# Gated linear attention and an ELU feed-forward layer on one core: blocks of 384 tokens instead of 256 from the fourth block on

## The chip, the cores and the metric

The kernel runs on one core of a Trainium2 chip. The metric is the device time of one execution in microseconds (us). The kernel before took 470.91 us, the median of three runs (469.48 to 471.95).

## The reference

Four sequences of 768 tokens pass through a linear attention of 8 heads of 48 with a gate for each step, and the 3072 resulting rows of 384 numbers through a feed-forward layer of width 2048. All arrays are float32.

```python
for t in range(S):                                   # S = 768, for every sequence b and head h
    state = alpha[:, :, t, :, None] * state + k_t (outer) v_t      # 48 x 48
    y[:, :, t] = q_t @ state
x = y.transpose(0, 2, 1, 3).reshape(3072, 384)
h = x @ w_in                                         # 384 x 2048
g = where(h > 0, h, exp(min(h, 0)) - 1)
out = g @ w_out                                      # 2048 x 384
```

## The kernel before, in words

**Tiling.** The attention works in 24 windows of 128 tokens (6 to a sequence), the feed-forward layer in 12 blocks of 256 tokens, two windows each. Every float32 product of the layer is made of three products in fp32r: each operand is split in an upper part and a rest, and rest times rest is left out.

**Steps.** The program is written as tokens, one small function each, called with a window or with a block `b` and a step `j`. A token issues its instructions on the engines' queues, and each queue runs in the order of the tokens. For a window: `L`, `LV` load it, `SC` scans the gates (VectorE), `LN`, `EX`, `PC` are ScalarE's, `KA`, `KB`, `KC`, `SQ` scale k and q (GpSimd and VectorE), `T` transposes k on VectorE in four parts of four instructions (line 296), `S` makes the scores (line 335) and `U` the products of k and v (line 380) on TensorE, both into two banks called q, `MK` masks the scores (line 363), `UA`, `UB`, `UC` bring the state forward (lines 417, 446), `Y` makes the rows of y (line 464; `YL`, `Y3` and `XP` help in the first four windows), and `XH`, `XL`, `XD` write them, split, into the block's tile `xt`.

For a block, the 2048 features are cut in 8 steps `j` of 256. `A(b, j)` (line 656) makes h for 256 features and 256 tokens: 2 groups of 128 features, 9 matmuls each of 256 columns (3 parts of the 384 inputs, 3 products each), both groups in one bank. `RA`, `RB` (lines 673, 678, ScalarE) make exp(min(h, 0)), `RC` (line 684, VectorE) the activation g, `GH` (line 690, ScalarE) its upper part, `GL` (line 704; VectorE, for the pairs in the table `GQS` GpSimd) the rest. `O(b, j)` (line 718) multiplies by w_out: for each of 2 groups of 128 tokens 6 matmuls of 384 columns, summed over all `j` in one bank per group, so two banks of the eight. `Z` (lines 727, 730) copies the two banks out, through tiles `ot` of which there are two, and stores them; the last block's stores go out on ScalarE's queue, the others on SyncE's.

**Order.** The string `START` writes out the tokens of blocks 0 to 3 with their windows and the arrival of the weights (`F` loads a piece, `KW`, `DA`, `DB`, `WH`, `WL` unpack and split it). After it `steady()` repeats the string `STEADY` once per block. The string `BANKS` gives the PSUM bank of every tile in turn, and a tile waits until the one before it in its bank is done with.

```python
def steady(g0=4):
    for g in range(g0, g0 + 10):
        for x in STEADY.split():
```

Of the kernel before, what the change touches and what calls it, by code (L numbers as in the profile page):

```python
# [24 lines left out]
NBLK = B * S // BLK  # L25
# [14 lines left out]
WLV, KAV, KBV, SQV = (0, 1, 2, 3, 4, 7, 8, 9, 13, 14, 15), (0, 1, 2, 6), (0, 1, 2, 3, 4, 10), (0, 1, 3, 6, 10)  # L40
# [3 lines left out]
GQS = ((0, 1), (0, 4), (0, 5), (0, 6), (0, 7), (1, 1), (1, 5), (1, 7), (2, 1), (2, 3), (2, 4), (2, 5), (2, 7), (3, 0), (3, 2), (3, 3), (3, 4))  # L44
# [9 lines left out]
DB.2 WH.4 A.0.0 RA.0.0 ZV.6 TP.3 DA.1 WL.4 KN.3 F.7 DA.3 WH.6 PC.2 XP.2 LV.3 RB.0.0 UC.2 S.3 MK.3 U.3 L.4 KW.3 A.0.2  # L54
WL.6 UA.3 F.10 YL.3 F.9 Y3.3 RC.0.0 GH.0.0 RA.0.2 XL.2 RB.0.2 DB.1 RA.0.1 SC.4 DB.3 F.8 Y.3 XH.3 RB.0.1 XL.3 RC.0.1
LV.6 F.12 A.0.3 WH.1 SQ.4 WH.5 WL.5 DA.4 GH.0.1 KW.4 F.14 A.1.0 UB.3 GL.0.1 GL.0.0 LV.5 RC.0.2 GH.0.2 RA.1.0 WL.1 WH.3
A.1.1 LN.4 EX.4 RB.1.0 GL.0.2 L.5 PC.3 A.1.3 UC.3 RA.1.1 WL.3 DB.4 RA.1.3 SC.5 RC.1.0 WH.8 WL.8 RB.1.1 A.1.2 RA.1.2
RB.1.2 SQ.5 RC.1.1 O.0.0 O.0.1 O.0.2 RC.1.2 KA.4 A.1.4 KB.4 F.11 RB.1.3 RC.1.3 GH.1.1 GH.1.0 GL.1.0 GL.1.1 O.1.0 WH.7
DA.5 WL.7 RA.0.3 RB.0.3 RC.0.3 WH.10 LN.5 O.1.1 GH.1.2 GL.1.2 O.1.2 EX.5 KC.4 GH.0.3 GL.0.3 O.0.3 DA.6 RA.1.4 GH.1.3
RB.1.4 GL.1.3 LC.1 WL.10 LV.7 A.0.5 KA.5 KB.5 KW.5 DB.5 KW.6 RA.0.5 A.0.4 RB.0.5 DB.6 RC.1.4 WH.11 RA.0.4 RB.0.4 O.1.3  # L60
RC.0.4 GH.1.4 GH.0.4 RC.0.5 WH.9 KC.5 A.1.5 WL.11 RA.1.5 WH.12 S.4 GL.1.4 RB.1.5 PC.5 S.5 GL.0.4 TP.4 KN.4 WL.12 WL.9
RC.1.5 L.6 GH.1.5 O.0.4 MK.5 U.4 WH.14 TP.5 PC.4 L.7 GH.0.5 GL.0.5 MK.4 O.1.4 SC.6 KN.5 F.13 LN.6 EX.6 WL.14 A.1.7
# [12 lines left out]
TB.10 GL.3.3 GL.3.4 O.2.7 KC.11 TB.11 TA.11 LC.4 L.12 Z.2 PC.10 LV.11
# [20 lines left out]
def gla_elu_ffn(ctx: ExitStack, tc: tile.TileContext, qka, vv, vn, wgt, out):  # L96
# [84 lines left out]
    @tok  # L181
    def L(i):
        t = qtile(i)
        nc.sync.dma_start(out=t, in_=qka[i, :, 0:QW])
# [282 lines left out]

    def xs(i):
        blk, half = divmod(i, 2)
        if blk not in xt:  # L470
            xt[blk] = xpool.tile([128, 2, NC, 2, W], F32R, name="xt", tag="xt")
        return xt[blk][:, half]
# [180 lines left out]

    @tok
    def A(b, j):
        x = xt[b]
        h = bank("h").rearrange("p (f x) -> p f x", f=2)
        ff[b, j] = dict(h=h)
        for f in range(2):
            k = 0  # L660
            t = wgts[2 * j]
            for c in range(NC):
                ws = slice(f * DM + c * 128, f * DM + c * 128 + 128)
                for wi, xi in ((0, 0), (0, 1), (1, 0)):
                    nc.tensor.matmul(h[:, f, :], lhsT=t[:, wi, ws], rhs=x[:, :, c, xi].rearrange("p a x -> p x a"),  # L665
                                     start=(f == 0 and k == 0), stop=(k == 8), skip_group_check=True)
                    k += 1

    @tok
    def RA(b, j):  # L670
        d = ff[b, j]
        r = d["r"] = gpool.tile([128, 2, BLK], F32, name="r", tag="r", bufs=3)
        nc.scalar.activation(out=r, in_=d["h"], func=AF.Relu, scale=-1.0)  # L673
# [6 lines left out]
    @tok  # L680
    def RC(b, j):
        d = ff[b, j]
        d["g"] = d["r"] if (b, j) in GQS else d["h"]
        nc.vector.scalar_tensor_tensor(out=d["g"], in0=d["r"], scalar=-1.0, in1=d["h"], op0=ALU.add, op1=ALU.max)  # L684

    @tok
    def GH(b, j):
        d = ff[b, j]
        gh = d["gh"] = gpool.tile([128, 2, BLK], F32R, name="gh", tag="gh", bufs=3)
        nc.scalar.copy(out=gh, in_=d["g"])  # L690

    @tok
    def GP(b, j):
        rest(ff[b, j]["h"], ff[b, j]["gh"])

    @tok
    def GL(b, j):
        d = ff[b, j]
        gl = d["gl"] = gpool.tile([128, 2, BLK], F32R, name="gl", tag="gl", bufs=3)
        if (b, j) in GPE:  # L700
            nc.scalar.copy(out=gl, in_=d["h"])
        else:
            q = nc.gpsimd if (b, j) in GQS else nc.vector
            q.tensor_tensor(out=gl, in0=d["g"], in1=d["gh"].bitcast(F32), op=ALU.subtract)  # L704

    @tok
    def O(b, j):
        d = ff.pop((b, j))
        gh, gl = d["gh"], d["gl"]
        if j == 0:  # L710
            ops_[b] = [bank("o") for _ in range(2)]
        for m in range(2):
            o = ops_[b][m]
            ms = slice(m * 128, m * 128 + 128)
            for f in range(2):
                t = wgts[2 * j + 1]
                for k, (gt, wi) in enumerate(((gh, 0), (gh, 1), (gl, 0))):
                    nc.tensor.matmul(o[:, 0:DM], lhsT=gt[:, f, ms],  # L718
                                     rhs=t[:, wi, f * DM:f * DM + DM].rearrange("p (a x) -> p x a", a=2),
                                     start=(j == 0 and f == 0 and k == 0),  # L720
                                     stop=(j == NJ - 1 and f == 1 and k == 2))

    @tok
    def Z(b):
        for m in range(2):
# [4 lines left out]
            q.dma_start(out=out[b * BLK + m * 128:b * BLK + m * 128 + 128, :], in_=ot)  # L730
        del ops_[b], xt[b]
# [43 lines left out]
def steady(g0=4):  # L775


    p, steps, last = [], dict(A=29, RA=29, RB=29, RC=29, GH=29, GL=29, O=27), NBLK * NJ
    for g in range(g0, g0 + 10):
        for x in STEADY.split():  # L780
            x, k, *y = x.split(".")
            if x in steps:
                k = NJ * g + int(k)
                if steps[x] <= k < last:
                    p.append((x, *divmod(k, NJ)))
            elif x in ("CA", "CB", "LC"):
                k = 4 * g + int(k)
                if 4 + (x == "LC") <= k < 4 * NJ:
                    p.append((x, k))
            elif x == "Z":  # L790
                if g0 - 1 <= g + int(k) < NBLK:
                    p.append((x, g + int(k)))
            elif x in ("V", "VP"):
                if g == NBLK - 1:
                    p.append((x,))
            elif 2 * g + int(k) < NWIN:
                p.append((x, 2 * g + int(k), *map(int, y)))
    return p


def general(ctx, tc, ident, whi, wlo, flag, qka, vn, wgt, out):
# [4 lines left out]
    with tc.If(good < 1):  # L806
        with ExitStack() as st:
# [177 lines left out]
```

## Time and profile before

| | us |
|---|---|
| runs of the kernel before, median (lowest to highest) | 470.91 (469.48 to 471.95) |
| the profiled execution, its own time | 471.73 |
| its span, first to last instruction | 470.0 |
| TensorE busy in the span | 461.1 (98%) |
| VectorE busy | 369.2 (79%) |
| ScalarE busy | 314.6 (67%) |
| GpSimd busy | 133.9 (28%) |
| granted TensorE clock, mean | 0.998 of 2.4 GHz |

The span is what the profiler saw between the first and the last instruction; 1.7 us of the execution's time lie around it. Matmuls are pipelined, so the duration of one says little: what one costs is the distance from start to start in a row of them, which the chain of waits gives as the length of a piece divided by its count. The other engines' rows give the mean duration of an instruction.

### The profile page before, as it was taken

Reading aid. Unit: us, or ns where it says so; the run is one execution under the profiler, and the core shown is the slowest. Engines: PE = TensorE matmul, PEld = TensorE weight load, DVE = VectorE, ACT = ScalarE, POOL = GpSimd, SP = SyncE. Lnnn points to the kernel's source line nnn. Section 1 sums busy time; section 2 is a strip of 40 time slices with the busy share of each in tenths; the row PEclk is TensorE's granted clock in tenths of the full one; section 3 lists DMA queues with packets and bytes.
Section 4 is the critical chain, followed back from the end, with each engine's and each line's share of the span. In section 5 each row is a group of like instructions: output and inputs, shape, how many; then the busy total and the mean of one; then the engine's idle time right before and its main releaser. Section 6 shows DMA issues by size and latency. Waiting matters only on the chain.

```text
span 470.0 us, 13140 instructions
## 1 busy us (share of the span) xinstructions
PE 461.1 (98%) x5413; PEld 446.1 (95%) x5414; DVE 369.2 (79%) x763; ACT 314.6 (67%) x664; POOL 133.9 (28%) x114
## 2 busy tenths in 40 slices
PE   8999999999999999999999999999999999999994
PEld 3899999999999999999999999999999999999994
DVE  7899978797959889789889889789899897334430
ACT  4789988685746566866865875767775865663550
POOL 2116545265544414403502602602602500000000
PEclk9999999999999999999999999999999999999999
DMA  8999704414070175246227236326325222110001
GB/s 309 398 415 354 242 1 153 153 52 165 16 210 2 39 231 189 68 122 201 69 85 234 71 92 214 85 85 214 93 77 177 68 77 78 33 44 10 2 35 38
DMA packets 20482, 61.12 MB, mean 130 GB/s; under 512 B 2880, under 2 KB 7872, under 8 KB 20416
## 3 DMA queue, kind: packets, MB, share of 16 engines
q1 hardware_dynamic: 20128, 59.82, 38.4%
q8 instruction: 44, 0.72, 0.7%
q10 hardware_dynamic: 288, 0.39, 0.2%
q14 instruction: 22, 0.18, 0.1%
HBM read 53.52 MB, written 4.72 MB: 124 GB/s over the span
## 4 chain that ended last, share of the span: by engine, by line
PE 98%; DVE 0%; ACT 0%; issue 0%
PE h L665 42%; PE o L718 40%; PE y L464 4%; PE q L380 2%; PE q L335 2%; PE y L459 2%; PE wp L137 2%; PE sc L351 1%; PE tp L286 1%; PE y L504 1%; PE u L398 1%; PE yl L459 1%; PE u L424 0%; PE y L523 0%; PE xf L137 0%
## 5 line engine op out<-in xcount | busy, mean ns | idle before, releaser
L665 PE MATMUL h<-xt,w 128*128 128x256 f32 x1728 | 201.2, 276 | 0.0
L665 PEld LDWEIGHTS h<-xt,w 128*128 128x128 f32 x1728 | 197.6, 192 | 0.9
L718 PE MATMUL o<-w,gh 128*128 128x384 f32 x768 | 188.8, 328 | 0.0
L718 PEld LDWEIGHTS o<-w,gh 128*128 128x128 f32 x768 | 132.6, 189 | 0.8
L718 PE MATMUL o<-w,gl 128*128 128x384 f32 x384 | 125.3, 326 | 0.0
L673 ACT ACTIVATE r<-h 128x512 f32<-128x512 f32 x96 | 56.1, 596 | 55.2 <-PE h L665 52.9
L296 DVE STREAM_TRANSPOSE kn<-qka 32x128 f32<-32x128 f32 x256 | 77.5, 303 | 4.0
L684 DVE SCALAR_TENSOR_TENSOR h<-r,h 128x512 f32<-128x512 f32 x79 | 53.8, 692 | 26.6 <-ACT r L678 26.1
L718 PEld LDWEIGHTS o<-w,gl 128*128 128x128 f32 x384 | 72.6, 189 | 0.1
L704 DVE TENSOR_TENSOR gl<-h,gh 128x512 fp32r<-128x512 f32 x79 | 54.0, 689 | 18.6 <-ACT gh L690 15.8
L690 ACT CAST gh<-h 128x512 fp32r<-128x512 f32 x79 | 45.8, 579 | 32.1 <-DVE h L684 19.7
L235 POOL TENSOR_TENSOR qka<-qka,R 128x512 f32<-128x512 f32 x20 | 26.8, 1342 | 137.9 <-ACT R L227 101.8
L678 ACT ACTIVATE r<-r 128x512 f32<-128x512 f32 x96 | 60.4, 631 | 1.8
L265 POOL TENSOR_TENSOR st<-qka,P 64x512 f32<-64x512 f32 x32 | 40.7, 1271 | 27.0 <-DVE P L213 17.4
L363 DVE TENSOR_TENSOR st<-q,mask 64x256 f32<-64x256 f32 x72 | 30.3, 421 | 8.0 <-PE q L335 6.8
L213 DVE TENSOR_TENSOR_SCAN P<-qka,first 128x516 f32<-128x516 f32 x24 | 30.5, 1269 | 5.5 <-DMA qka<-in_qka_dram 5.1
L222 ACT ACTIVATE R<-P 128x512 f32<-128x512 f32 x24 | 15.1, 630 | 28.9 <-DVE P L213 28.9
L704 POOL TENSOR_TENSOR gl<-r,gh 128x512 fp32r<-128x512 f32 x17 | 24.4, 1438 | 25.8 <-ACT gh L690 18.6
L240 POOL TENSOR_TENSOR R<-P,R 128x512 f32<-128x512 f32 x18 | 23.3, 1296 | 10.9 <-DVE qka L235 9.6
L615 ACT ACTIVATE ck<-ck,lim 128x384 int32<-128x384 int8 x32 | 24.1, 755 | 2.2 <-DMA ck<-in_wgt_dram 2.2
L620 ACT ACTIVATE ck<-ck,lim 128x384 f32<-128x384 int32 x32 | 22.9, 715 | 0.8
L464 PEld LDWEIGHTS y<-st,vs 128*64 128x64 f32 x576 | 18.0, 138 | 2.5 <-issue 2.3
(95 smaller groups left out, 430.2 us busy)
## 6 DMA issues: line engine op xcount, KB each, us to landing
qka<-in_qka_dram SPq DMA_DIRECT2D x22, 770.0 KB, 6.1
ck<-in_wgt_dram SPq DMA_DIRECT2D x32, 384.0 KB, 3.6
raw<-in_wgt_dram SPq DMA_DIRECT2D x16, 767.6 KB, 9.8
vs<-in_vv_dram SPq DMA_DIRECT2D x36, 192.0 KB, 4.3
out_dram<-ot SPq DMA_DIRECT2D x22, 192.0 KB, 2.0
vs<-in_vv_dram SPq DMA_DIRECT2D x6, 384.0 KB, 7.0
xt<-y SPq DMA_DIRECT2D x40, 48.0 KB, 2.2
qka<-in_qka_dram SPq DMA_DIRECT2D x2, 512.0 KB, 5.0
```

Of the source, the lines that this page charges most:

```text
L213: nc.vector.tensor_tensor_scan(out=P.rearrange("p n w -> p (n w)"), data0=t[:, 2 * NP * W:], data1=first.rearrange("p n w -> p (n w)"), in ...
L265: eng(SQV, i).tensor_tensor(out=st[r, a], in0=d["q"][r], in1=pw(i)[r], op=ALU.mult)
L296: nc.vector.transpose(out=kn[32 * t:32 * t + 32, :, 32 * g:32 * g + 32], in_=d["kt"][32 * g:32 * g + 32, :, 32 * t:32 * t + 32])
L363: nc.vector.tensor_tensor(out=d["st"][r, a, :, c * C:(c + 1) * C], in0=d["s4"][a][o], in1=mask[o].unsqueeze(1).broadcast_to([64, NP, C]), ...
L464: nc.tensor.matmul(out[64 * a:64 * a + m], lhsT=lhs(i, c, a)[:, n * D:n * D + m], rhs=d["st"][:, a, n, c * C:(c + 1) * C], start=start, st ...
L665: nc.tensor.matmul(h[:, f, :], lhsT=t[:, wi, ws], rhs=x[:, :, c, xi].rearrange("p a x -> p x a"), start=(f == 0 and k == 0), stop=(k == 8) ...
L673: nc.scalar.activation(out=r, in_=d["h"], func=AF.Relu, scale=-1.0)
L678: nc.scalar.activation(out=d["r"], in_=d["r"], func=AF.Exp, scale=-1.0)
L684: nc.vector.scalar_tensor_tensor(out=d["g"], in0=d["r"], scalar=-1.0, in1=d["h"], op0=ALU.add, op1=ALU.max)
L690: nc.scalar.copy(out=gh, in_=d["g"])
L704: q.tensor_tensor(out=gl, in0=d["g"], in1=d["gh"].bitcast(F32), op=ALU.subtract)
L718: nc.tensor.matmul(o[:, 0:DM], lhsT=gt[:, f, ms], rhs=t[:, wi, f * DM:f * DM + DM].rearrange("p (a x) -> p x a", a=2), start=(j == 0 and f ...
```

## The change

From block 3 on a block has 384 tokens, three windows, so that there are 3 blocks of 256 and 6 of 384. In a wide block a step `j` is one group of 128 features: there are 16 steps, `A` makes one h of 128 x 384 with 9 matmuls of 384 columns, the elementwise tokens work on 128 x 384, and `O` has 3 groups of 128 tokens with 3 matmuls each, in three banks. The tables are rewritten: `STEADY` now holds one wide block, `START` holds blocks 0 to 2 and twelve steps of block 3, `BANKS` follows. In a wide block `GL` is GpSimd's for 5 of the 16 steps (`GQW`). Some of the early windows' `KA`, `KB`, `SQ` and some weights' `WL` change between VectorE and GpSimd. The tiles r, gh and gl, three of each before, share ten. `xt` is laid out in another order, so that a row that `XD` moves is cut in six pieces. The loads of the last four windows are issued in two parts. `Z` copies three banks, each as a token of its own. A fallback that does not run with these inputs (`general`) is rewritten for both widths.

```diff
+NARROW = 3
+WIDE = 384
+NBLK = NARROW + (B * S - NARROW * BLK) // WIDE
-WLV, KAV, KBV, SQV = (0, 1, 2, 3, 4, 7, 8, 9, 13, 14, 15), (0, 1, 2, 6), (0, 1, 2, 3, 4, 10), (0, 1, 3, 6, 10)
+WLV, KAV, KBV, SQV = (0, 2, 3, 4, 8, 10, 11, 12), (0, 1, 2, 4, 7, 8), (0, 1, 2, 3, 5, 9), (0, 1, 3, 5)
+GQW = (2, 5, 8, 11, 14)
...
-            xt[blk] = xpool.tile([128, 2, NC, 2, W], F32R, name="xt", tag="xt")
+            xt[b] = xpool.tile([128, NC, 2, WIDE], F32R, name="xt", tag="xt")
...
+    def parts(b, j):
+        return ((j // 2, j % 2),) if wide(b) else ((j, 0), (j, 1))
+    def gtile(b, dt, name):
+        return cut(b, gpool.tile([128, 512], dt, name=name, tag="g", bufs=10))
...
     def A(b, j):
-        for f in range(2):
+        for y, (p, f) in enumerate(parts(b, j)):
...
-                    nc.tensor.matmul(h[:, f, :], lhsT=t[:, wi, ws], rhs=x[:, :, c, xi].rearrange("p a x -> p x a"),
+                    nc.tensor.matmul(h[:, y, :], lhsT=t[:, wi, ws],
+                                     rhs=x[:, c, xi].rearrange("p (a x) -> p x a", a=2),
...
     def O(b, j):
-            ops_[b] = [bank("o") for _ in range(2)]
+            ops_[b] = [bank("o") for _ in range(2 + wide(b))]
...
-    def Z(b):
-        for m in range(2):
+    def Z(b, *ms):
+        for m in ms or range(2):
             ot = gpool.tile([128, DM], F32, name="ot", tag="ot")
             nc.scalar.copy(out=ot, in_=ops_[b][m][:, 0:DM])
```

**Where the instructions move.** TensorE, steady part, around the small products of the windows (q is written by `S`, line 335, and `U`, line 380; y by `Y`, line 464). Before, two windows' `Y` stand together, and elsewhere two windows' `U` and `S`:

```order
L718 MATMUL o<-w_695,gl 128x384
L464 MATMUL y<-st,vs_121 64x64 x16
L464 MATMUL y<-st,vs_120 64x64 x16
L665 MATMUL h<-xt,w_1070 128x256 x18
...
L380 MATMUL q<-vs_118,kn 48x48 x16
L335 MATMUL q<-st,qka_133 64x64 x16
L380 MATMUL q<-vs_119,kn 48x48 x16
L335 MATMUL q<-st,qka_134 64x64 x16
L718 MATMUL o<-w_1023,gh 128x384 x2
```

The same engine and part of the changed kernel, where `S` is line 349, `U` line 394, `Y` line 478, `A` line 701 and `O` line 747:

```order
L747 MATMUL o<-w_863,gl 128x384
L478 MATMUL y<-st,vs_120 64x64 x16
L349 MATMUL q<-st,qka_133 64x64 x16
L394 MATMUL q<-vs_121,kn 48x48 x16
L747 MATMUL o<-w_863,gh 128x384 x2
```

Each stop now serves one window's `Y` and another window's `S` and `U`, three stops to a wide block of three windows.

VectorE, steady part, the transposes `T` (kn, line 296) of two windows before the scores. Before:

```order
L704 TENSOR_TENSOR gl<-h,gh 128x512
L296 STREAM_TRANSPOSE kn<-qka_133 32x4x32 x4
L296 STREAM_TRANSPOSE kn<-qka_134 32x4x32 x4
L541 TENSOR_TENSOR y_4541<-y,y_4541 128x128
L545 TENSOR_TENSOR xt<-y,xt 128x3x128
```

The changed kernel, the transposes of the window whose `S` and `U` stand in the stop shown above (transposes line 310, `RC` line 721, `GL` line 734, `KC` line 259, `XL` line 568, `MK` line 377):

```order
L568 TENSOR_TENSOR xt<-y,xt 128x3x128
L259 SCALAR_TENSOR_TENSOR qka_133<-R,qka_133 128x512
L721 SCALAR_TENSOR_TENSOR h<-r,h 128x384
L310 STREAM_TRANSPOSE kn<-qka_133 32x4x32 x4
L734 TENSOR_TENSOR gl<-h,gh 128x384
L310 STREAM_TRANSPOSE kn<-qka_133 32x4x32 x4
L721 SCALAR_TENSOR_TENSOR h<-r,h 128x384
L734 TENSOR_TENSOR gl<-h,gh 128x384
L310 STREAM_TRANSPOSE kn<-qka_133 32x4x32 x4
L721 SCALAR_TENSOR_TENSOR r<-r,h 128x384
L734 TENSOR_TENSOR gl<-h,gh 128x384
L310 STREAM_TRANSPOSE kn<-qka_133 32x4x32 x4
```

The transposes now stand between the elementwise steps of the block, and the last four come right ahead of the stop that needs them.

ScalarE, the end of the program (copies and stores of the last block, with what each waits for; DMAHW is a DMA's semaphore). Before:

```order
L690 CAST gh<-h 128x512 [waits PE_49]
L727 COPY ot<-o 128x384 [waits DMAHW0_49,PE_49]
L730 DMA out_dram<-ot 128x384 [waits Activation_49]
L727 COPY ot<-o 128x384 [waits DMAHW1_49,PE_49]
L730 DMA out_dram<-ot 128x384 [waits Activation_49]
```

The changed kernel (copy line 757, store line 760):

```order
L757 COPY ot<-o 128x384 [waits DMAHW3_49,PE_49]
L760 DMA out_dram<-ot 128x384 [waits DMAHW5_49,Activation_49]
L757 COPY ot<-o 128x384 [waits DMAHW4_49]
L760 DMA out_dram<-ot 128x384 [waits DMAHW6_49,Activation_49]
L757 COPY ot<-o 128x384 [waits DMAHW5_49,PE_49]
L760 DMA out_dram<-ot 128x384 [waits Activation_49]
```

There is a third copy and store, and the third copy takes the `ot` tile of the first.

## Rows read from the trace of the kernel before

**Rows 1.** The page, busy time of each engine.

```profile
PE 461.1 (98%) x5413; PEld 446.1 (95%) x5414; DVE 369.2 (79%) x763; ACT 314.6 (67%) x664; POOL 133.9 (28%) x114
```

**Rows 2.** Waits of TensorE, the one past its start: waiter, releaser, us in total, times, longest.

```profile
PE y L504 <- ACT y L492: 0.4, 1, 0.4
```

**Rows 3.** Chain that ended last: start us, length us, what, matmuls.

```profile
57.84 2.28 PE o L718 x14
...
262.23 7.80 PE o L718 x48
270.03 2.02 PE y L464 x64
272.05 6.22 PE h L665 x54
...
280.22 0.51 PE q L380 x32
...
447.89 6.03 PE h L665 x54
...
463.68 0.03 issue
```

**Rows 4.** Timeline of TensorE at the start of a stop: start us, length us.

```profile
269.71 0.33 PE L718 MATMUL o<-w,gl 128*128 128x384 f32 x1
269.96 0.28 PE L464 MATMUL y<-st,vs 128*64 128x64 f32 x2
```

**Rows 5.** Groups by form: busy us, mean ns of one, idle before.

```profile
L678 ACT ACTIVATE r<-r 128x512 f32<-128x512 f32 x96 | 60.4, 631 | 1.8
L690 ACT CAST gh<-h 128x512 fp32r<-128x512 f32 x79 | 45.8, 579 | 32.1 <-DVE h L684 19.7 <-PE o L718 12.1
L519 ACT ACTIVATE xt<-y 128x384 fp32r<-128x384 f32 x24 | 12.0, 500 | 1.5 <-PE y L459 1.5
L704 DVE TENSOR_TENSOR gl<-h,gh 128x512 fp32r<-128x512 f32 x79 | 54.0, 689 | 18.6 <-ACT gh L690 15.8 <-POOL R L240 0.8 <-PE o L718 0.7
L545 DVE TENSOR_TENSOR xt<-y,xt 128x384 fp32r<-128x384 f32 x21 | 11.5, 548 | 0.0
L704 POOL TENSOR_TENSOR gl<-r,gh 128x512 fp32r<-128x512 f32 x17 | 24.4, 1438 | 25.8 <-ACT gh L690 18.6 <-PE y L464 3.9 <-PE q L335 3.2
```

**Rows 6.** Busy time by stretch, the mean of three blocks: us, busy us by engine.

```profile
sum 107.78, PE 107.78 PEld 106.02 DVE 95.50 ACT 75.58 POOL 30.56; mean PE 35.93 PEld 35.34 DVE 31.83 ACT 25.19 POOL 10.19
```

**Rows 7.** Timeline of VectorE, one window's work: start us, length us.

```profile
269.88 3.79 DVE L296 STREAM_TRANSPOSE kn<-qka 32x128 f32<-32x128 f32 x12
...
274.38 2.53 DVE L296 STREAM_TRANSPOSE kn<-qka 32x128 f32<-32x128 f32 x8
...
281.26 0.86 DVE L363 TENSOR_TENSOR st<-q,mask 64x256 f32<-64x256 f32 x2 [0.99 <-PE q L335]
...
285.12 1.22 DVE L213 TENSOR_TENSOR_SCAN P<-qka,first 128x516 f32<-128x516 f32 x1
```

**Rows 8.** Timelines of ScalarE and VectorE ahead of the first product of block 1.

```profile
54.26 0.58 ACT L690 CAST gh<-h 128x512 fp32r<-128x512 f32 x1
...
55.43 0.69 DVE L704 TENSOR_TENSOR gl<-h,gh 128x512 fp32r<-128x512 f32 x1
```

**Rows 9.** Timeline of ScalarE at the end, then each store's us to landing.

```profile
462.73 0.48 ACT L727 COPY ot<-o 128x384 f32<-128x384 f32 x1 [4.45 <-PE o L718]
463.24 0.38 ACTq L730 DMA_DIRECT2D out_dram<-ot  x1
...
464.22 0.34 ACTq L730 DMA_DIRECT2D out_dram<-ot  x1
...
DMA to landing us min/median/max: 1.9/1.9/1.9
...
DMA to landing us min/median/max: 4.1/4.1/4.1
```

**Rows 10.** The page, DMA issues: count, KB each, us to landing.

```profile
xt<-y SPq DMA_DIRECT2D x40, 48.0 KB, 2.2
```

More of the change, by code (lines that the diff above doesn't have):

```diff
@@ L58 @@
[L58 to L62, printed above, removed]
@@ L183, in L @@
         t = qtile(i)
-        nc.sync.dma_start(out=t, in_=qka[i, :, 0:QW])
+        cuts = (0, NP * W, QW) if i >= NWIN - 4 else (0, QW)
+        for x, y in zip(cuts, cuts[1:]):
+            nc.sync.dma_start(out=t[:, x:y], in_=qka[i, :, x:y])
     @tok
@@ L466, in ymm, with block, wide @@
                          start=start, stop=True, skip_group_check=True)
+    def block(i):
+        if i < 2 * NARROW:
+            return divmod(i, 2)
+        b, a = divmod(i - 2 * NARROW, 3)
+        return NARROW + b, a
+    def wide(b):
+        return int(b >= NARROW)
     def xs(i):
-        blk, half = divmod(i, 2)
-        if blk not in xt:
-            xt[blk] = xpool.tile([128, 2, NC, 2, W], F32R, name="xt", tag="xt")
-        return xt[blk][:, half]
+        b, a = block(i)
+        if b not in xt:
+            xt[b] = xpool.tile([128, NC, 2, WIDE], F32R, name="xt", tag="xt")
+        return xt[b][:, :, :, a * W:(a + 1) * W]
     @tok
@@ L652, in gla_elu_ffn, with cut, inr @@
     ff, ops_ = {}, {}
+    def parts(b, j):
+        return ((j // 2, j % 2),) if wide(b) else ((j, 0), (j, 1))
+    def cut(b, t):
+        return t[:, 0:WIDE].unsqueeze(1) if wide(b) else t.rearrange("p (f x) -> p f x", f=2)
+    def gtile(b, dt, name):
+        return cut(b, gpool.tile([128, 512], dt, name=name, tag="g", bufs=10))
+    def inr(b, j):
+        return j in GQW if wide(b) else (b, j) in GQS
     @tok
     def A(b, j):
-        x = xt[b]
-        h = bank("h").rearrange("p (f x) -> p f x", f=2)
+        x = xt[b][:, :, :, 0:WIDE if wide(b) else BLK]
+        h = cut(b, bank("h"))
         ff[b, j] = dict(h=h)
-        for f in range(2):
+        for y, (p, f) in enumerate(parts(b, j)):
             k = 0
-            t = wgts[2 * j]
+            t = wgts[2 * p]
             for c in range(NC):
@@ L664, in A @@
                 for wi, xi in ((0, 0), (0, 1), (1, 0)):
-                    nc.tensor.matmul(h[:, f, :], lhsT=t[:, wi, ws], rhs=x[:, :, c, xi].rearrange("p a x -> p x a"),
-                                     start=(f == 0 and k == 0), stop=(k == 8), skip_group_check=True)
+                    nc.tensor.matmul(h[:, y, :], lhsT=t[:, wi, ws],
+                                     rhs=x[:, c, xi].rearrange("p (a x) -> p x a", a=2),
+                                     start=(y == 0 and k == 0), stop=(k == 8), skip_group_check=True)
                     k += 1
@@ L698, in GL @@
         d = ff[b, j]
[L699 to L704, printed above, removed]
+        gl = d["gl"] = gtile(b, F32R, "gl")
+        q = nc.gpsimd if inr(b, j) else nc.vector
+        q.tensor_tensor(out=gl, in0=d["g"], in1=d["gh"].bitcast(F32), op=ALU.subtract)
     @tok
@@ L710, in O @@
         if j == 0:
-            ops_[b] = [bank("o") for _ in range(2)]
-        for m in range(2):
-            o = ops_[b][m]
+            ops_[b] = [bank("o") for _ in range(2 + wide(b))]
+        for m, o in enumerate(ops_[b]):
             ms = slice(m * 128, m * 128 + 128)
-            for f in range(2):
-                t = wgts[2 * j + 1]
+            for y, (p, f) in enumerate(parts(b, j)):
+                t = wgts[2 * p + 1]
                 for k, (gt, wi) in enumerate(((gh, 0), (gh, 1), (gl, 0))):
-                    nc.tensor.matmul(o[:, 0:DM], lhsT=gt[:, f, ms],
+                    nc.tensor.matmul(o[:, 0:DM], lhsT=gt[:, y, ms],
                                      rhs=t[:, wi, f * DM:f * DM + DM].rearrange("p (a x) -> p x a", a=2),
-                                     start=(j == 0 and f == 0 and k == 0),
-                                     stop=(j == NJ - 1 and f == 1 and k == 2))
-    @tok
-    def Z(b):
-        for m in range(2):
+                                     start=(j == 0 and y == 0 and k == 0),
+                                     stop=(p == NJ - 1 and f == 1 and k == 2))
+    @tok
+    def Z(b, *ms):
+        row = NARROW * BLK + (b - NARROW) * WIDE if wide(b) else b * BLK
+        for m in ms or range(2):
             ot = gpool.tile([128, DM], F32, name="ot", tag="ot")
@@ L729, in Z @@
             q = nc.sync if b < NBLK - 1 else nc.scalar
-            q.dma_start(out=out[b * BLK + m * 128:b * BLK + m * 128 + 128, :], in_=ot)
-        del ops_[b], xt[b]
+            q.dma_start(out=out[row + m * 128:row + m * 128 + 128, :], in_=ot)
+            if m == 1 + wide(b):
+                del ops_[b], xt[b]
     flag = []
@@ L772, in gla_elu_ffn, with steady @@
     general(ctx, tc, ident, [t[:, 0] for t in wgts], [t[:, 1] for t in wgts], flag[0], qka, vn, wgt, out)
-def steady(g0=4):
-    p, steps, last = [], dict(A=29, RA=29, RB=29, RC=29, GH=29, GL=29, O=27), NBLK * NJ
-    for g in range(g0, g0 + 10):
+def steady():
+    p, done = [], set(START.split())
+    for i in range(NWIN):
+        if f"MK.{i}" in done:
+            done |= {f"MK.{i}.0", f"MK.{i}.1"}
+        if f"TP.{i}" in done or f"TA.{i}" in done:
+            done |= {f"T.{i}.{g}" for g in range(4)}
+    for g in range(-1, NBLK - NARROW + 1):
         for x in STEADY.split():
             x, k, *y = x.split(".")
[L782 to L785, printed above, removed]
+            if x in ("A", "RA", "RB", "RC", "GH", "GL", "O"):
+                k = 16 * g + int(k)
+                if 0 <= k < 16 * (NBLK - NARROW):
+                    p.append((x, NARROW + k // 16, k % 16))
             elif x in ("CA", "CB", "LC"):
-                k = 4 * g + int(k)
-                if 4 + (x == "LC") <= k < 4 * NJ:
+                k = 6 * g + int(k)
+                if 0 <= k < 4 * NJ:
                     p.append((x, k))
             elif x == "Z":
-                if g0 - 1 <= g + int(k) < NBLK:
-                    p.append((x, g + int(k)))
+                k = NARROW + g + int(k)
+                if NARROW <= k < NBLK:
+                    p.append((x, k, *map(int, y)))
             elif x in ("V", "VP"):
-                if g == NBLK - 1:
+                if g == NBLK - NARROW - 1:
                     p.append((x,))
-            elif 2 * g + int(k) < NWIN:
-                p.append((x, 2 * g + int(k), *map(int, y)))
-    return p
+            elif 0 <= 2 * NARROW + 3 * g + int(k) < NWIN:
+                p.append((x, 2 * NARROW + 3 * g + int(k), *map(int, y)))
+    return [x for x in p if ".".join(map(str, x)) not in done]
 def general(ctx, tc, ident, whi, wlo, flag, qka, vn, wgt, out):
```

184 lines of the change are left out of this document (99 added, 85 removed).

## The prediction

> **What bounds the kernel now.** I read the shares first: TensorE is busy 98% of the span, no other engine over 79% [rows 1]. A busy TensorE can still be a waiting one, so I looked at its waits: past the start there is one, of 0.4 us [rows 2]. Then the chain that ended last: it runs along TensorE without a break into the last output product, and its pieces have constant prices. 54 h matmuls take 6.03 us, 111.7 ns each for 256 columns; 48 output matmuls take 7.80 us, 162.5 ns each for 384 columns [rows 3]. Per column that is 0.436 against 0.423 ns, so narrow ones cost 3% more. The time is therefore TensorE's work, plus what lies behind its last matmul (ended near 463.68 us) until the stores have landed.
>
> **The change, part by part.** The sum is made against the profiled execution, 471.73 us, which is 0.82 us over the median of the runs, 470.91.
>
> *h products.* Blocks 0 to 2 keep theirs. The nine others had 9 x 8 x 18 = 1296 matmuls of 256 columns: 1296 x 111.7 ns = 144.8 us. Six wide blocks have 6 x 16 x 9 = 864 of 384 columns; at the price of an output matmul of that width, 162.5 ns, 140.4 us [rows 3]. **-4.36 us.** The output products are 864 of 384 columns either way and cost the same.
>
> *Stops for the windows' small products.* A stop costs more than its products. Entering: the last output matmul starts at 269.71 and the first y matmul at 269.96, 0.09 us beyond the 0.16 of that matmul [rows 4]. Leaving: 54 h matmuls behind a stop take 6.22 us, 54 elsewhere 6.03 [rows 3], 0.19 more. Together 0.28 us. In the order of TensorE I count 27 such stops in the kernel before and 29 in the changed one, behind the warm-up: **+0.56 us.** In 12 of the 29 a full-height y product now meets a half-height q product. No row shows that meeting in the steady part; the bounds are nothing and a whole stop's 0.28 us, 0 to +3.4 us in all. I take the 0.09 of entering, the nearest single change of shape: **+1.08 us.**
>
> *The end.* Before, each of the two banks has six matmuls in the last step, so the first copy starts 0.95 us ahead of TensorE's end E = 463.68, its store is issued 0.51 us behind the copy's start and lands 1.9 us later; the second is issued at E+0.54 and lands 4.1 us later [rows 9]. Now each of three banks has three matmuls. The order copies the middle bank first: it is done 0.49 us ahead of E, so the copy starts at E-0.46, its store is issued at E+0.05 and lands at E+1.95. The third copy takes the same `ot` tile and cannot start earlier, although its bank is done at E: issue at E+2.46, 1.92 us later than the last issue before. If the last store again takes 4.1 us, **+1.92 us**; with 1.9 us it is -0.3. I take the first, since the last store in the row is the one with 4.1.
>
> *Early waits.* The 0.4 us wait [rows 2] is for ScalarE's copy between `YL.3` and `Y.3`. Now `A.0.3`, 2 us, stands between: **-0.4 us.** The reordered weights and early windows I cost at nothing, and this is the cover: before `O.1.0`, which began at 57.84 [rows 3], its last input came from VectorE at 56.12 and ScalarE's part of it at 54.84 [rows 8], 1.7 us to spare. In the new order TensorE has two tokens less ahead of it (`O.0.2`, `A.1.4`: 4.0 us), VectorE five tokens and a `KB` less and a `KA` and a `KB` more (about 3.7 us less), ScalarE seven less and four more (about 2.0 us less). By VectorE 1.5 us are left, by ScalarE 53.5 against 53.9, 0.4 us. Without that cover it costs what is late, 0 to 2 us.
>
> *Elementwise work.* More, smaller instructions. For a wide block take 1.5 blocks of before [rows 6], remove 12 of each of the 128 x 512 forms (0.6 us on ScalarE, 0.69 on VectorE) and add 16 (for `GL` on VectorE 11) at 384 columns, 500 ns on ScalarE and 548 on VectorE [rows 5]. ScalarE: 37.8 - 21.6 + 24.0 = 40.2 us; VectorE: 47.7 - 16.6 + 14.8 = 46.0 us; GpSimd at most 15.3 + 5 x 1.44 = 22.5 us. TensorE has 53.9 - 0.73 + 0.18 = 53.3 us of work in that time, so 75%, 86% and 42%; before, 70%, 89% and 28%. No engine becomes the bound by its sum, so nothing is added. What is late next is VectorE in one stretch (rival A).
>
> *Transfers.* `XD`'s rows come in six pieces; a landing took 2.2 us [rows 10], and between the last `XL` of a block and the next block's first `A` TensorE has five steps, 7.3 us. Shared tiles, split loads and the fallback have no instruction on TensorE's path.
>
> Sum: 471.73 - 4.36 + 0.56 + 1.08 + 1.92 - 0.4 = 470.53; 0.82 less against the median: **469.7 us**, a gain of 1.2 us, under the 0.5% (2.35 us) that a measurement of this kernel can tell from no change. Its own range is 467.5 (the last store lands in 1.9 us) to 471.7 (the early cover is gone).
>
> **The rivals.**
>
> *A: `U` waits for the transposes (slower).* Before, the last transposes ended at 276.9, 3.3 us ahead of the `U` of 280.22 [rows 3, 7]. Now, from the end of one window's `S` to the next stop's `U`, VectorE must do `MK`, `UA`, `UB`, `UC` (3.9 us from 281.26 to 285.12), the scan 1.22, `XL` and `KC` 1.3 by the nearest forms, 16 transposes at 316 ns, 5.05, and seven elementwise steps, 3.84 [rows 5, 7]: 15.3 us. TensorE meanwhile has nine steps of 1.46 us, 13.2, two y (1.0 each, half of 2.02), a `U` and an `S` (0.5 each) [rows 3] and 0.4 for leaving and entering stops: 16.6 us. 1.3 us to spare, some 1.0 if signals take 0.3. It decides once VectorE idles more than 1 us there. It idles 11% of a block now [rows 6], which would be 1.9 us here: 0.9 late, at four windows +3.6; one elementwise step of 0.55 us more ahead of them at two of the four, +1.1: 474.4 us. Against it: its idle time is mostly waiting for others with nothing owed, and here it is behind. For it: nothing in the trace has so little to spare.
>
> *B: no price for the mixed stops, and the last store lands as fast as the first (faster).* 469.7 - 1.08 - 2.2 = 466.4 us. For it: 1.9 us is the only other landing of such a store [rows 9].
>
> *C: the excess stays with h.* 111.7 ns is 5 ns over 256 columns at 2.4 GHz, 162.5 is 2.5 over 384. If h's extra 2.5 belongs to its operands and not its width, 864 x 2.5 ns = 2.2 us come back and the change does half of what it says: 471.9 us. The Trainium skill (TensorE: Matmul & The Clock Gate, section Back-to-back issue gap) gives 2.5 ns over the columns at any width: the row of 384 columns agrees, that of 256 does not (111.7, not 109.2). Against C: nothing else differs between the two rows than width and operand.
>
> *D: a bank short.* `A.8` of a wide block takes a bank of the window's scores 4.7 us of TensorE's work after `S`, and VectorE needs 4.0 us to be done with it. Two elementwise steps ahead of it, 1.1 us, make 0.4 us late at five blocks, +2.0: 471.7 us. The Trainium skill (Perfetto Trace Analysis, Optimization Strategy) reads a repeating gap on the engine that should be saturated as too little SBUF or PSUM, which speaks against a third output bank; before, with two, no such gap is in the waits [rows 2].
>
> **How the numbers follow.** Forecast 0.46, A 0.18, B 0.20, C 0.08, D 0.08. Faster by over 0.5%, below 468.56: B, and 0.10 of the forecast, where its last store lands early, 0.30. Slower, above 473.26: A, 0.18. Within: 0.52. The range reaches from B's 466.4 to just short of A's 474.4: 466.4 to 474.2.
>
> **What would show it.** In the chain, 9 h matmuls of 384 columns in 1.46 us (C: 1.49). TensorE's waits near zero; under A a wait of `U` on VectorE's transposes, four times; under D one of `A` on VectorE, five times. At the end a ScalarE copy that waits 1 us for a DMA, and the last issue about 2.5 us behind the last matmul. The forecast is wrong if TensorE's work falls by other than 2.5 to 4 us, or if waits of more than 1.5 us appear on it.

## The result, and the profile after

The changed kernel takes **474.61 us**, the median of 6 runs (474.07 to 475.03), the kernel before 470.62 on the same chip (6 runs, 469.48 to 471.96). The ratio is 1.0081, 95% interval 1.0059 to 1.0104: slower by 0.8%. The profiled execution took 474.70 us with a span of 473.0, 3.0 us more than before; the medians lie 4.0 apart, because the profiled execution of before (471.73) was 1.1 us above the median of these six.

The page, busy time by engine, to be set beside [rows 1]:

```profile
PE 461.0 (97%) x4982; PEld 443.3 (94%) x4982; DVE 358.4 (76%) x781; ACT 320.1 (68%) x736; POOL 163.9 (35%) x144
```

TensorE has 431 instructions fewer and is as long busy as before; a busy row of a matmul that is pipelined says little, as ever. No other engine is near a bound. So the waits come next. TensorE's waits (waiter, releaser, us in total, times, longest), which answer to [rows 2]:

```profile
PE q L394 <- DVE st L377: 2.5, 6, 0.5
PE wp L149 <- DVE first L143: 2.1, 1, 2.1
PE y L473 <- issue: 0.3, 1, 0.3
PE tp L300 <- PE h L701: 0.2, 1, 0.2
```

The first row is new. `U` (line 394) waits six times for VectorE, and what it waits for is `MK` (line 377), the mask, not the transposes (line 310). The second row stands in both kernels: the start. The wait of [rows 2] is gone.

TensorE at one of the four places, the second stop of the pattern (start us, length us):

```profile
218.27 0.33 PE L747 MATMUL o<-w,gl 128*128 128x384 f32 x1
218.52 0.69 PE L349 MATMUL q<-st,qka 48*64 48x64 f32 x32
219.75 0.28 PE L394 MATMUL q<-vs,kn 64*48 64x48 f32 x2 [0.53 <-DVE st L377]
220.20 0.57 PE L394 MATMUL q<-vs,kn 64*48 64x48 f32 x30 [0.16 <-DVE st L377]
220.70 1.15 PE L478 MATMUL y<-st,vs 128*64 128x64 f32 x32
221.78 0.43 PE L701 MATMUL h<-xt,w 128*128 128x384 f32 x1
```

And VectorE at the same time:

```profile
216.88 1.26 DVE L310 STREAM_TRANSPOSE kn<-qka 32x128 f32<-32x128 f32 x4
218.17 1.02 DVE L734 TENSOR_TENSOR gl<-h,gh 128x384 fp32r<-128x384 f32 x2
219.27 0.88 DVE L377 TENSOR_TENSOR st<-q,mask 64x256 f32<-64x256 f32 x2
```

The transposes are done at 218.14, before `S` begins. `S` is through at 219.2; then the two halves of the mask run, 0.44 us each. `U` starts its first product behind the first half and the rest behind the second (each of these float32 products shows as two matmuls, so the row's x2 is one product; at two of the four places `U` serves a sequence's last window, has half its products and waits for the first half of the mask alone). The stop's small products take 3.26 us, from 218.52 to 221.78. In the third stop of the pattern, where `U` stands ahead of the mask, they take 2.07:

```profile
235.14 1.15 PE L478 MATMUL y<-st,vs 128*64 128x64 f32 x32
236.22 0.69 PE L349 MATMUL q<-st,qka 48*64 48x64 f32 x32
236.74 0.54 PE L394 MATMUL q<-vs,kn 64*48 64x48 f32 x32
237.21 0.59 PE L747 MATMUL o<-w,gh 128*128 128x384 f32 x2
```

The h products, for [rows 3], 18 of them in the timeline:

```profile
414.38 3.09 PE L701 MATMUL h<-xt,w 128*128 128x384 f32 x18
417.31 0.49 PE L747 MATMUL o<-w,gh 128*128 128x384 f32 x2
```

From start to start 2.925 us for 18, 162.5 ns each: the price that was forecast.

ScalarE at the end and the last store's landing, for [rows 9]:

```profile
468.06 0.48 ACT L757 COPY ot<-o 128x384 f32<-128x384 f32 x1 [1.05 <-SPq L843]
468.57 0.34 ACTq L760 DMA_DIRECT2D out_dram<-ot  x1
...
DMA to landing us min/median/max: 2.6/2.6/2.6
```

The third copy waits 1.05 us; its store lands at 471.2.

Taking for every row of TensorE the distance to the next row's start, the two traces differ like this; TensorE's last matmul ends at 466.05 instead of 463.67:

| TensorE's time | before, us | after, us | difference |
|---|---|---|---|
| h products at their price | 192.97 | 188.64 | -4.33 |
| output products at their price | 187.04 | 187.04 | 0 |
| waits of `U` for the mask, four stops over 2.07 us | 0 | 3.87 | +3.87 |
| other small products after 62 us | 44.38 | 45.32 | +0.94 |
| entering and leaving stops, waits between large products | 5.61 | 6.79 | +1.18 |
| small products before 62 us | 22.43 | 23.63 | +1.20 |
| warm-up products | 8.83 | 8.36 | -0.47 |

(The 3.87 is what the first experiment took away; the four stops show 3.83.) The sum is +2.39, and behind the last matmul another 0.6 us is lost, 6.93 against 6.36 up to the span's end.

### The profile page after: what moved, and what is told of

Its sections match the earlier page's. It is cut to its first block, busy times and chain, and to the rows that moved or that the text cites. A ratio compares the mean times of both kernels' runs of the same rounds, so it can differ in the third digit from the quotient of the medians.

```text
span 473.0 us, 12461 instructions
## 1 busy us (share of the span) xinstructions
PE 461.0 (97%) x4982; PEld 443.3 (94%) x4982; DVE 358.4 (76%) x781; ACT 320.1 (68%) x736; POOL 163.9 (35%) x144
## 5 line engine op out<-in xcount | busy, mean ns | idle before, releaser
L701 PE MATMUL h<-xt,w 128*128 128x384 f32 (+1 forms) x1296 | 202.9, 311 | 0.0
L701 PEld LDWEIGHTS h<-xt,w 128*128 128x128 f32 x1296 | 191.1, 190 | 1.3
L710 ACT ACTIVATE r<-h 128x384 f32<-128x384 f32 (+1 forms) x120 | 61.4, 513 | 86.2 <-PE h L701 85.9
L734 POOL TENSOR_TENSOR gl<-r,gh 128x384 fp32r<-128x384 f32 (+1 forms) x43 | 50.5, 1175 | 184.2 <-DVE h L721 59.5
L721 DVE SCALAR_TENSOR_TENSOR h<-r,h 128x384 f32<-128x384 f32 (+1 forms) x77 | 44.4, 578 | 37.3 <-ACT r L715 36.7
L715 ACT ACTIVATE r<-r 128x384 f32<-128x384 f32 (+1 forms) x120 | 64.6, 548 | 1.6
L734 DVE TENSOR_TENSOR gl<-h,gh 128x384 fp32r<-128x384 f32 (+1 forms) x77 | 43.8, 575 | 23.2 <-ACT gh L727 21.4
L727 ACT CAST gh<-h 128x384 fp32r<-128x384 f32 (+1 forms) x77 | 37.4, 494 | 8.9 <-DVE h L721 7.3
L721 DVE SCALAR_TENSOR_TENSOR r<-r,h 128x384 f32<-128x384 f32 (+1 forms) x43 | 25.4, 590 | 6.8 <-ACT r L715 6.5
L727 ACT CAST gh<-r 128x384 fp32r<-128x384 f32 (+1 forms) x43 | 23.6, 549 | 8.2 <-DVE r L721 5.7
```

Source lines behind the costliest of these rows:

```text
L701: nc.tensor.matmul(h[:, y, :], lhsT=t[:, wi, ws], rhs=x[:, c, xi].rearrange("p (a x) -> p x a", a=2), start=(y == 0 and k == 0), stop=(k = ...
L715: nc.scalar.activation(out=d["r"], in_=d["r"], func=AF.Exp, scale=-1.0)
```

## The experiments

**1. `U` ahead of the mask.** In the second stop:

```diff
-S.5 MK.5.1 U.5
+S.5 U.5 MK.5.1
```

The order of instructions on every engine is the same with and without this edit; the tokens stand on different engines. What it turns is which of the two waits for the other, since both touch the two banks that `S` has written.

> The changed kernel with U ahead of its window's mask MK in the second stop of the pattern (S U MK in place of S MK U). No engine's own order of instructions changes; only which of the two waits for the other. Theory M (U waits for the mask, because both touch the banks that S has just written): the four long stops (3.26, 2.80, 3.25, 2.80 us of small products) shrink to the 2.07 us of the other mixed stops, -3.8 us: 470.8 us, ratio to the kernel before 0.998 to 1.003, and the gaps of 0.75 us between S and U are gone. Rival T (VectorE is late with the transposes, the rival A of the prediction): U's wait stays and is put down to the transposes, 474 to 475 us, ratio 1.007 to 1.009. Rival V (the mask, now behind U, makes VectorE late elsewhere): the gap moves to another step of TensorE, 472 to 474 us.

Measured: 470.58 us, median of 12 runs (469.89 to 471.35), ratio to the kernel before 0.9985 (0.996 to 1.001). Against the changed kernel, 4.0 us less. Theory M holds, T and V fall. The waits of TensorE that are left:

```profile
PE wp L149 <- DVE first L143: 2.1, 1, 2.1
PE tp L300 <- PE h L701: 0.2, 1, 0.2
```

and the same stop, with 2.06 us between 217.90 and 219.96:

```profile
217.90 0.69 PE L349 MATMUL q<-st,qka 48*64 48x64 f32 x32
218.41 0.54 PE L394 MATMUL q<-vs,kn 64*48 64x48 f32 x32
218.88 1.15 PE L478 MATMUL y<-st,vs 128*64 128x64 f32 x32
219.96 0.76 PE L701 MATMUL h<-xt,w 128*128 128x384 f32 x3
```

The wait has gone over to VectorE, where nothing was late (VectorE's timeline):

```profile
219.00 0.86 DVE L377 TENSOR_TENSOR st<-q,mask 64x256 f32<-64x256 f32 x2 [0.47 <-PE q L394]
```

**2. The same wait put into the kernel before.** In its `STEADY`:

```diff
-CB.-12 U.2 XD.1 S.2 MK.2.0 UA.2
+CB.-12 XD.1 S.2 MK.2.0 U.2 UA.2
```

> The kernel before, with U of the even window put behind S and the first half of the mask (S MK U in place of U S MK), seven times in the steady pattern; nothing else moves. Theory M: each of the seven stops gets the wait that the changed kernel has at its second stop, 0.7 to 1.2 us: +5.1 to +8.3 us, 475.7 to 479 us, ratio 1.011 to 1.018. Rival (the wait costs only because the wide pattern makes VectorE late): under 1 us, ratio 0.999 to 1.003.

Measured: 478.29 us (4 runs, 477.63 to 479.68), ratio 1.0161 (1.0124 to 1.0197). Theory M again: the wait belongs to the order `S MK U` and not to the wide blocks. Waits and one of the seven stops:

```profile
PE q L380 <- DVE st L363: 4.9, 14, 0.5
```

```profile
284.52 0.69 PE L335 MATMUL q<-st,qka 48*64 48x64 f32 x32
285.74 0.28 PE L380 MATMUL q<-vs,kn 64*48 64x48 f32 x2 [0.52 <-DVE st L363]
286.19 0.80 PE L380 MATMUL q<-vs,kn 64*48 64x48 f32 x42 [0.17 <-DVE st L363]
```

The row gives 4.9 us for 14 waits, but the stops grew from 1.82 to 3.01 us, 8.3 us for seven. A wait's row is the idle time that is left behind modelled ends of pipelined matmuls; what a wait costs is read from start to start. The profiled execution as a whole is only 6.9 us longer than that of before, although its TensorE ends 9.1 us later: its last store landed sooner (experiment 6).

**3. The `y` products apart.** Experiment 1, and one large step put between `Y` and the window's `S` and `U` in each stop, for instance:

```diff
-MK.4.1 Y.3 A.3
+MK.4.1 A.3 Y.3
```

> The kernel with U ahead, and in each of the three stops of the pattern one step of 9 or so large products is put between the y products and the window's S and U: twelve more stops, and none of them mixes the two kinds. By the stop's price that the trace of the changed kernel shows (0.19 us of entering and leaving, a mixed stop's products 0.15 us dearer than the same products apart): 12 x (0.19 - 0.15) = +0.5 us against the kernel with U ahead, 471.3 us. By the prediction's prices (0.28 a stop, 0.09 a mixing): 12 x (0.28 - 0.09) = +2.3 us, 473.1 us. If mixing costs nothing: 12 x 0.19 = +2.3 us as well, and the stops' products then show the same sum as before.

Measured: 473.88 us (6 runs, 473.62 to 475.42), ratio 1.0069 (1.0042 to 1.0096), 3.3 us over experiment 1, more than any of the three sums. The trace divides it. The second stop, now two:

```profile
218.97 0.69 PE L349 MATMUL q<-st,qka 48*64 48x64 f32 x32
219.48 0.54 PE L394 MATMUL q<-vs,kn 64*48 64x48 f32 x32
219.95 1.73 PE L701 MATMUL h<-xt,w 128*128 128x384 f32 x9
221.61 1.15 PE L478 MATMUL y<-st,vs 128*64 128x64 f32 x32
222.69 0.43 PE L747 MATMUL o<-w,gh 128*128 128x384 f32 x1
```

0.98 us of q products (218.97 to 219.95) and 1.08 of y (221.61 to 222.69): 2.06, the same as when they stood together. So mixing the two kinds costs nothing, and a stop more costs 0.20 us of entering and leaving (2.38 us for twelve). Another 0.8 us are two new waits of an h product for the mask (line 377), and 0.15 us lie in the first of these stops, where the edit parts `S` from `U`.

**4. `Y` between `S` and `U`.** Experiment 1, with the same number of stops and three runs of products in each:

```diff
-S.5 U.5 MK.5.1 CB.4 LC.5 RC.7 GH.5 UA.5 Y.4
+S.5 Y.4 U.5 MK.5.1 CB.4 LC.5 RC.7 GH.5 UA.5
```

> The kernel with U ahead, and in each of the three stops of the pattern the y products are put between S and U in place of beside them: twelve stops as before, each with three unbroken runs of small products in place of two. Theory G (an unbroken run costs 0.14 us beyond its products): the stops' small products grow from 2.07 to 2.21 us, +1.7 us, 472.3 us. Rival (the number of changes of kind inside a stop counts, at the prediction's 0.09 us): 2.16 us, +1.1 us, 471.7 us. Rival (neither; only the number of stops counts, 0.20 us each): 2.07 us, no change, 470.6 us.

Measured: 474.38 us (6 runs, 474.09 to 475.71), ratio 1.0086 (1.0059 to 1.0113). The time is no answer: in the profiled execution another 3.5 us are lost between large products, most of it ahead of h products that wait for the mask or for `XD`'s rows (the longest, 1.1 us), which come later. The stop's rows are one:

```profile
218.52 0.69 PE L349 MATMUL q<-st,qka 48*64 48x64 f32 x32
219.14 1.15 PE L478 MATMUL y<-st,vs 128*64 128x64 f32 x32
220.22 0.57 PE L394 MATMUL q<-vs,kn 64*48 64x48 f32 x32
220.73 0.43 PE L701 MATMUL h<-xt,w 128*128 128x384 f32 x1
```

2.21 us, as theory G has it, where experiment 1 had 2.06 with the same 96 products. (Eleven of the twelve stops changed so, since the first is written in `START`; all small products behind 62 us grew by 1.6 us.) Going from `S` to `U` costs nothing extra, going from q to y or back does: an unbroken run of one kind costs 0.14 us beyond its products. The rows show the array's shapes, 48\*64 and 64\*48 for q, 128\*64 for y, 128\*128 for the large ones. The Trainium skill (TensorEngine Tiling (Array Packing), section Key Properties) says that a change of tiling mode drains TensorE; by that rule q and y are two modes and `S` and `U` one, which the trace agrees with, some 0.14 to 0.17 us a change (a stop with one run has two of them, 0.20 and 0.14 us).

**5. Two windows' `y` together.** To have one run fewer, `Y.3` was moved from the first stop to the second, beside `Y.4`:

```diff
-MK.4.1 Y.3 A.3 RA.2 O.-3 XH.3 MK.4.0
+MK.4.1 A.3 RA.2 O.-3 MK.4.0
-UA.5 Y.4 A.6
+UA.5 Y.3 XH.3 Y.4 A.6
```

> The kernel with U ahead, and the first window's y products taken out of the first stop of the pattern and put directly ahead of the second window's y in the second stop, four times; the number of stops stays. Theory G (each unbroken run of one kind of small products costs some 0.14 us beyond its products, wherever it stands): one run fewer in each of four rounds, -0.56 us: the two stops hold 0.98 and 3.01 us of small products in place of 2.07 and 2.07; 470.0 us. Rival (the small products cost the same in any grouping): 1.0 and 3.1 us, no change of the sum, 470.6 us. Rival W (the later x rows, 13 us closer to the block that reads them, make its first h wait): a new gap before an h product, time above 470.6 us.

Measured: 492.56 us (6 runs, 491.67 to 493.67), ratio 1.0454 (1.0426 to 1.0482). A miss, and not for one of the reasons expected. TensorE's waits and the stop:

```profile
PE y L478 <- DVE vs L460: 9.2, 2, 4.6
PE y L478 <- DVE st L377: 6.0, 2, 3.0
```

```profile
217.60 0.54 PE L394 MATMUL q<-vs,kn 64*48 64x48 f32 x32
222.73 3.42 PE L478 MATMUL y<-st,vs 128*64 128x64 f32 x64 [4.59 <-DVE vs L460]
```

`Y.3` kept its bank, and at its new place `S` of the same stop has just taken that bank, so that `Y` waits for the window's mask and state steps. These waits are not the whole of it: the four stops are 20.7 us longer, of which some 15.4 us are waits. In the other 5.3 us TensorE runs at a lower clock. After 4.6 us of idling its granted clock, 1.00 up to 217 us, is near the lower of its two levels (1.2 and 2.4 GHz), and the 64 y matmuls take 3.35 us instead of the 2.02 of [rows 3]; from 226 us on it is 1.00 again. This stretch by engine, the granted clock third from the end:

```profile
222.73:226.08 3.35, 3.35 (x65) 3.28 (x65) 1.59 (x3) 0.84 (x4) 0.00 (x0) 0.56 0.02 5
```

Another bank is hard to find: the string of banks has three for the output, two for q, two for y and one for an h that is still read there, all eight. Theory G was not tested by this run, since the stop is full of waits.

**6. The end.** Three edits on the last block. A tile of its own for the third copy (on experiment 1):

```diff
-            ot = gpool.tile([128, DM], F32, name="ot", tag="ot")
+            ot = (gtile(b, F32, "ot")[:, 0] if b == NBLK - 1 and m == 2
+                  else gpool.tile([128, DM], F32, name="ot", tag="ot"))
```

> As the kernel with U ahead, and in the last block the third copy of the output takes a tile of its own instead of the first copy's. Theory (the third copy waits 1.05 us for the first store, and the end is as late): the third copy starts right behind the second, the last store is issued 1.0 us earlier and the time falls by 0.8 to 1.1 us against the kernel with U ahead: about 469.8 us. Rival (the three stores share what carries them, and the last lands when the bytes are through): the issue comes 1.0 us earlier, its landing takes as much longer, and the time falls by under 0.3 us.

Measured: 470.40 us (12 runs, 469.70 to 473.56), ratio 0.9995 (0.9976 to 1.0014): no difference to experiment 1 that can be measured. Then the first and third bank copied by VectorE and stored on SyncE's queue, with that tile:

```diff
+            if last and m != 1:
+                nc.vector.tensor_copy(out=ot, in_=ops_[b][m][:, 0:DM])
...
+            q = nc.scalar if last and m == 1 else nc.sync
```

> The kernel with U ahead, and in the last block the first and the third bank of the output are copied by VectorE and stored by SyncE's queue, the middle one by ScalarE as before; three tiles. Theory (what sets the end is that copies and issues stand one behind the other on ScalarE, 0.93 us a pair, and that the third copy waits for the first store): the last issue falls from E+2.5 to about E+0.6 us (E: the end of the last output product), and with landings of 2.3 to 3.7 us the span ends at E+4.8 to E+5.5 in place of E+6.8: -1.3 to -2.0 us, 468.6 to 469.3 us, ratio to the kernel before 0.994 to 0.997. Rival (the landings grow as the stores come closer together, as the second's 3.4 to 4.1 us do): the span ends at E+6.0 or later, under -0.8 us.

Measured: 470.71 us (12 runs, 469.86 to 470.96), ratio 1.000 (0.9983 to 1.0018). The last issue did come at E+0.6 instead of E+2.5, and nothing came of it. ScalarE at the end of experiment 1, then VectorE and the queues here:

```profile
463.58 0.48 ACT L757 COPY ot<-o 128x384 f32<-128x384 f32 x1 [1.05 <-SPq L843]
464.09 0.34 ACTq L760 DMA_DIRECT2D out_dram<-ot  x1
```

```profile
461.82 1.31 SPq L765 DMA_DIRECT2D out_dram<-ot  x2
462.21 0.56 DVE L760 COPY ot<-o 128x384 f32<-128x384 f32 x1 [0.42 <-PE o L747]
...
DMA to landing us min/median/max: 3.9/3.9/3.9
```

The last store is issued at 462.8, 0.6 us behind the last matmul's end, and lands 3.9 us later, at 466.7. In experiment 1 the last was issued at 464.1 (E+2.5) and took 2.3 us, to 466.4. What the DMA engines moved here, in 40 slices of 0.19 us from 461.5 on:

```profile
GB/s 0 0 0 0 0 0 295 393 393 393 393 377 377 464 213 0 0 0 44 0 8 8 8 16 25 0 0 0 0 0 0 87 0 0 0 0 0 44 0 0
```

The three stores' data go out in one stretch, done by 464.3, and the last landing is 2.4 us behind it. Counted from each execution's own last matmul, the last issue moved from E+2.5 to E+0.6 and the last landing from E+4.9 to E+4.5. The times keep to the bounds that both rivals gave, and the theory's gain of 1.3 to 2.0 us is out. That the stores share what carries them, the rivals' reason, is not shown. Experiment 2 speaks for another reading. Its end is that of the kernel before, instruction for instruction, and the last store is issued at E+0.56 in both; before, it landed 4.1 us later [rows 9], at E+4.7, and in experiment 2 at E+2.4:

```profile
473.35 0.34 ACTq L730 DMA_DIRECT2D out_dram<-ot  x1
...
DMA to landing us min/median/max: 1.8/1.8/1.8
```

So a landing differs by 2.3 us from one execution to another with nothing changed at the end, more than any of these edits was to give. Only the medians of many runs count here, and they are level.

Experiment 5 with the end changed as well (the first bank by VectorE and SyncE's queue, the third by ScalarE from its own tile):

```diff
+            if last and m == 0:
+                nc.vector.tensor_copy(out=ot, in_=ops_[b][m][:, 0:DM])
...
+            q = nc.sync if not last or m == 0 else nc.scalar
```

> As the kernel with the y pair, and at the end the second copy is made by VectorE and stored by SyncE's queue, the third by ScalarE into a tile of its own. Theory (copies and issues on one engine, 0.93 us apart, set the last issue, and a store then lands in 1.9 to 3.7 us whatever else flies): the last issue falls from E+2.1 to E+1.0 us (E: the end of the last output product), the last landing from E+5.1 to about E+4.2 us, -0.9 us: 469.1 us, ratio to the kernel before 0.996. Rival (the stores share what carries them; the last one lands at E+4.6 to E+4.9 us as in the two kernels with earlier issues): -0.2 to -0.5 us.

Measured: 491.92 us (6 runs, 490.59 to 493.23), ratio 1.043 (1.0403 to 1.0456). It stands on experiment 5 and shares its 20 us, and the two kernels' times overlap (491.67 to 493.67 there). In its profile the last store was issued at E+1.0 and landed at E+4.05, as the theory had it; with the scatter that experiment 2 shows, one execution does not decide between theory and rival.

## Why the prediction was wrong

The forecast was no change, 469.7 us, with a range up to 474.2; the time was 474.6. Of the 4.9 us between, 0.7 come from the medians: the forecast took 0.82 us off the profiled execution, but that of the changed kernel lies only 0.1 us above its median. The rest is in the terms.

- **h products, -4.36: right.** -4.33, at 162.5 ns. Rival C is out. (The Trainium skill (TensorE: Matmul & The Clock Gate, section Back-to-back issue gap), which the prediction sets beside C, gives its 2.5 ns over the columns for an isolated matmul and has other figures for a stream. Here a stream at 384 columns kept to it.)
- **The step that failed: "Stops for the windows' small products".** It counted the stops and the changes of kind in them from TensorE's order alone, and gave no price to what stands between `S` and `U` in the program's order. In one stop of three that is `MK`, on VectorE, on the same two banks. Four times 0.73 to 1.19 us, 3.87 in all; without them the changed kernel is at 470.58, 0.9 us from the forecast.
- **Rival A named the right waiter and engine, the wrong releaser.** "`U` waits for the transposes", four times, 474.4 us. The time is near by chance: at the place shown the transposes were done 1.6 us ahead of `U`, and what it owed VectorE was the mask of its own window, which rival A's sum had put down as the work of the window before. (The 0.3 us that rival A set aside for signals stands in no row; here `U` starts 0.04 us behind the end of the first half of the mask.) Experiment 1 separates the two, since it leaves the transposes where they are.
- **Stops and mixed stops, +0.56 and +1.08: the size nearly, the reason wrong.** A stop costs 0.20 us, not 0.28, mixing as such costs nothing, and each run of one kind costs 0.14. (The 0.19 us of leaving came from two pieces of the chain, which run between modelled ends; from start to start the first h behind that stop takes 0.10 us more than the others, in the trace of before already.) Before, two windows had one run of y and one of q; now each window has both, 12 runs more, 1.7 us by experiment 4's price. The other small products behind 62 us became some 0.8 us cheaper, so that their row stands at +0.94. Of the +1.18 in the next row 0.5 belongs to the stops behind 62 us: 1.4 in all, in place of 1.6.
- **The end, +1.92: mis-sized.** The copy waited 1.05 us for the first store as forecast and was issued at E+2.5, but its store landed in 2.6 us, not 4.1. It cost 0.6 us. One trace could not choose between the 1.9 and the 4.1 us of the prediction: the same last store of before took 4.1 us in one execution and 1.8 in experiment 2.
- **Early waits and cover, -0.4 and 0: mis-sized.** The wait on `Y3` is gone, but the reordered start was not free. Up to 62 us the small products are 1.2 us dearer, of which 0.5 us is a gap at 23.2 us that is absent in experiment 1, with the same `START`, and larger in experiment 4's profile; in experiment 1 they are 0.34 us dearer. The rest of the +1.18, 0.7 us, lies here too: two stops more, and the wait of `tp` for an h product.
- **Rival D** (a bank short) is not in the changed kernel's waits. In experiments 3 and 4 there is a wait of its kind, of an h product for the mask, twice each.
- **Elementwise work, 0:** right. From 200 to 250 us VectorE is busy 87%, ScalarE 70% and GpSimd 36% (86, 75 and 42 forecast), and no wait on them is left in experiment 1.

A round of a wide block in experiment 1 takes 53.59 us (second stops at 217.90, 271.49, 325.07, 378.67), 1.5 blocks of before 53.90 (35.93 us a block). The forecast had 53.3 [rows 6]. The wide block saves 0.73 us of h and gives 0.42 of it back, three runs of small products more.

No version beats both kernels by more than can be told: experiment 1 is 4.0 us faster than the changed kernel and level with the one before.

## What to carry to other kernels

Wherever two instructions of one engine touch a bank, look at what another engine does on that bank between them in the program's order: swapping two tokens can turn a wait round without moving one instruction on any queue, and it is worth turning it to the engine with slack. Count a tensor engine's small products in unbroken runs of one kind, as well as in stops. A saving of 3% on each product is small against one wait of a microsecond per round, so the order around the saved work needs the same care as the products.

## What the runs showed of the hardware

- `U` writes columns 0 to 191 of the two banks and `MK` reads columns 192 to 447, and still one waits for the other, 0.73 to 1.19 us a stop. The Trainium skill (PSUM — Partial Sum Buffer, section PSUM bank collisions raise a hardware error) asks for such guards by bank and 32-partition quadrant, not by address. Here the guard goes by the bank alone: `U`'s first product writes partitions 0 to 47 of the first bank and starts at 219.75, behind the half of the mask that reads partitions 64 to 127 of it up to 219.71. The wait in the rows is what that guard costs; no run here shows what happens without it, or with one by quadrant.
- A store of 192 KB to the output at the end landed in 1.8 to 4.1 us, and the same last store in 4.1 us before and in 1.8 us in experiment 2. What sets it stays open. With the last of three issued at E+0.6 instead of E+2.5 the time stayed, 470.71 against 470.58 us.
- Behind 4.6 us of idling the granted TensorE clock was 0.56 for 3.35 us, and 64 y matmuls took that long instead of 2.02 us (experiment 5): a long wait costs more than its length.
